# A two-layer linear-attention and SwiGLU kernel: the first row tile's keys by one fp32 product, four row tiles turned by TensorE, and new engine orders

## The chip, the cores and the metric

The kernel runs on one core of a Trainium2 chip. The metric is device time in microseconds for one execution, lower is better. The time before is 1136.47 us, the median of three runs (1135.8 to 1136.66).

## The reference

x has 2048 rows of 512. Two layers, each an attention block and a gated MLP, with the same weights in both layers:

```python
x = x + A(layernorm(x), wqkv, wo)     # linear attention, 32 heads of 16
x = x + B(layernorm(x), w1, w3, w2)   # silu(x@w1) * (x@w3) @ w2, 1792 hidden
# twice; in A:
pq, pk = phi(q), phi(k)               # phi(t) = (t+1 if t>0 else exp(t)) + 1e-6
kv  = einsum("bhsd,bhse->bhde", pk, v);  z = pk.sum over s
num = einsum("bhqd,bhde->bhqe", pq, kv); den = einsum("bhqd,bhd->bhq", pq, z) + 1e-6
out = (num / den) @ wo
```

All is fp32 in the reference.

## The kernel before

**Numbers as pairs.** A fp32 operand is held as two half-precision parts, high and low, after a scaling by a power of two. `mm` (L942) makes a product in three passes, `PASSES = ((0,0),(1,0),(0,1))`: high by high, low of the left by high, high of the left by low. Thus a 128 x 512 product over 512 inputs (four blocks k) is 12 matmuls of 512 columns. `split` (L835) makes the two parts of a weight: high on ScalarE, then low on VectorE.

**Scale of a weight.** `weight_scale` (L801): maxima of four pieces (`abs_max`, L788), a reduction (L805), a fp32 matmul against the identity into the bank `pm_k` (L808) to get the maximum over partitions, a reduction out of it (L810), a floor (L811), a scale (L813), and `flip_pow2` (L821), which turns it into the inverse power of two. Only then may `split` run.

**Row tiles.** The 2048 rows are 16 tiles of 128. Tile t needs its row statistics (`ln_stats`, VectorE L909 and L910, then four small GpSimd operations L917 to L921), `normalise` (ScalarE L924), a high part (ScalarE or GpSimd), a low part (a subtraction, GpSimd or VectorE), and it must be turned, so that its 512 inputs stand on the partitions. Tiles 0 and 1 are turned on TensorE (`first_tile`, L2342: four matmuls against the identity for each part into a bank `turn`, which ScalarE copies out, L2357); tile 2 by a transposing DMA (L939), all later ones by such a DMA in `keys_turn` (L1851, DMA L1858). All DMAs are issued on SP, whose order is fixed as well.

**Keys.** In `attention` (L1355), for each tile: the product of the turned tile with the keys' weights into a bank `pk` (12 matmuls), phi (`phi_act` L1333: Relu, Identity and Exp on ScalarE, where Identity writes back into the bank, so that the bank stays taken; `phi_sum` L1347: add and maximum on VectorE, L1350), the result's two parts (ScalarE L1396, VectorE L1405), and, a tile or two later, `gram`: 12 matmuls into the banks `gt`, which gather keys by rows over all tiles. Queries, the MLP, and a second layer that works on pairs of tiles follow.

**Banks.** PSUM's eight banks are two pools of four: `acc` (the `gt` and other sums) and `w` (tiles of ones, turns, `pm_k`, `pk`). A tile of the pool `w` can be written only when one of the four is free: when the last reader of what it held is done.

**Start.** Before the weights are there, `keep_busy` has TensorE multiply tiles of ones (L2369), 22 and later 3.

**Order.** The program is written in a plain order, and `arrange` then lays every engine's instructions out by a table `ORDER`: for each engine, the numbers of its instructions in program order, in the order in which they are to be issued. An engine issues strictly in that order, so an instruction that must wait holds all behind it. Nothing else sets the order.

Of the kernel before, what the change touches and what calls it, by code (L numbers as in the profile page):

```python
# [17 lines left out]
P = 128  # L18
# [477 lines left out]
def kernel(  # L496
# [833 lines left out]
    DEEP = 4  # L1330


    def phi_act(ps, u, eps, in_bank=False):  # L1333

# [1121 lines left out]
```

## Time and profile before

| | us |
|---|---|
| median of three runs | 1136.47 |
| span of the profiled execution | 1134.0 |
| outside the span, to the median | 2.5 |
| TensorE busy | 1123.7 (99%) |
| VectorE, ScalarE, GpSimd busy | 849.3, 663.2, 429.7 |
| TensorE's granted clock, mean | 0.999 |

A profile row gives start and length in us, the engine (PE is TensorE, DVE VectorE, ACT ScalarE, POOL GpSimd, SPq the queue of SP), the line of the kernel, the operation, out<-in by tile names, the shapes and a count; the bracket tells how long the engine was idle before it and what ended that. A row with a count is a run of equal instructions. A wait row reads: who waited, for whom, us in total, times, the longest. A row of a stretch gives its length and then, for TensorE, its weight loads, VectorE, ScalarE and GpSimd, the busy time with the count of instructions, the granted clock, the DMA engines' share and GB/s. A row of groups gives busy us and mean ns; a row of one tile gives shortest, median and longest duration in ns and the first and last start; a row of DMA issues gives KB and us from issue to landing.

### The profile page before, as it was taken

What the parts mean: (1) busy time and instruction counts of PE and PEld (TensorE: products, weight loads), DVE (VectorE), ACT (ScalarE), POOL (GpSimd) and SP (SyncE); (2) the same over time, 40 slices, a digit from 0 to 9 for tenths busy, and PEclk for the clock granted to TensorE, in tenths of its full rate; (3) what the DMA queues carried; (4) which work ended last, traced back from release to release, by engine and by line L of the source; (5) the groups of instructions that cost most, each with busy time, mean ns of one, the idle gap of its engine ahead of it and who ended that gap; (6) DMA issues with size and microseconds to landing.
All of it is one profiled execution on the core that took longest, in us unless ns stands there. A gap on an engine that the chain in (4) does not pass through costs nothing.

```text
span 1134.0 us, 22473 instructions
## 1 busy us (share of the span) xinstructions
PE 1123.7 (99%) x9117; PEld 888.3 (78%) x9117; DVE 849.3 (75%) x1468; ACT 663.2 (58%) x1104; POOL 429.7 (38%) x477
## 2 busy tenths in 40 slices
PE   8999999999999999999999999999999999999998
PEld 3445446888888888888886676578888888888887
DVE  7789878896978887889896488847855666465556
ACT  7668878775544445455578666686544434343442
POOL 6731796502001222335678416862152110302113
PEclk9999999999999999999999999999999999999999
DMA  8995665389673332331267946643482440220001
GB/s 258 304 292 181 174 136 121 75 220 272 204 279 122 117 149 103 112 155 66 48 179 177 276 165 153 114 89 105 120 240 102 177 178 1 85 84 29 11 20 57
DMA packets 171768, 162.94 MB, mean 144 GB/s; under 512 B 139536, under 2 KB 147984, under 8 KB 167056
## 3 DMA queue, kind: packets, MB, share of 16 engines
q1 hardware_dynamic: 171664, 161.51, 48.7%
q8 instruction: 71, 1.16, 0.4%
q14 instruction: 33, 0.27, 0.1%
HBM read 80.08 MB, written 47.32 MB: 112 GB/s over the span
## 4 chain that ended last, share of the span: by engine, by line
PE 91%; DVE 2%; POOL 2%; DMA 2%; issue 1%; ACT 1%; SPq 0%; DVEq 0%; POOLq 0%; ACTq 0%
PE bb L947 26%; PE po L2097 20%; PE bc L947 13%; PE ba L947 6%; PE gt L947 6%; PE po L947 5%; PE pq L947 4%; PE pk L947 3%; PE po L2117 3%; DMA arena<-arena 2%; PE kb L947 1%; PE qb L947 1%; PE kc L947 1%; PE kv L947 0%; PE qc L947 0%
## 5 line engine op out<-in xcount | busy, mean ns | idle before, releaser
L947 PEld LDWEIGHTS <-arena 128*128 128x128 f16 x6648 | 646.1, 98 | 204.5 <-DMA arena<-arena 4.4
L947 PE MATMUL bb<-arena 128*128 128x256 f16 x2688 | 349.2, 273 | 0.0
L2097 PE MATMUL po<-arena 128*128 128x256 f16 x2058 | 288.5, 273 | 0.0
L2052 ACT ACTIVATE arena<-bb 128x512 f32<-128x512 f32 x196 | 115.3, 594 | 195.5 <-PE bb L947 166.7
L2097 PEld LDWEIGHTS <-arena 128*128 128x128 f16 x2058 | 201.3, 98 | 23.4
L947 PE MATMUL bc<-arena 128*128 128x256 f16 x1344 | 179.6, 273 | 0.0
L2055 DVE TENSOR_TENSOR arena<-arena,bc 128x512 f32<-128x512 f32 x112 | 76.7, 685 | 87.5 <-PE bc L947 54.1
L2007 ACT ACTIVATE arena<-arena,scalars 128x512 f32<-128x512 f32 x112 | 74.6, 666 | 90.2 <-DVE arena L2055 70.2
L2146 DVE SCALAR_TENSOR_TENSOR arena<-po,scalars,arena 128x256 f32<-128x256 f32 (+1 forms) x180 | 101.5, 585 | 31.7 <-PE po L2097 21.7
L2013 DVE TENSOR_TENSOR arena<-arena 128x1280 f16<-128x1280 f32 (+1 forms) x90 | 105.4, 1174 | 21.2 <-ACT arena L2011 20.8
L2011 ACT ACTIVATE arena<-arena 128x512 f16<-128x512 f32 (+1 forms) x112 | 101.0, 904 | 32.2 <-DVE arena L2026 13.7
L2008 DVE SCALAR_TENSOR_TENSOR arena<-arena,scalars 128x512 f32<-128x512 f32 x112 | 78.6, 705 | 34.5 <-ACT arena L2007 34.4
L947 PE MATMUL ba<-arena 128*128 128x256 f16 x672 | 91.8, 273 | 0.0
L947 PE MATMUL gt<-arena 128*128 128x512 f16 x384 | 89.6, 379 | 0.0
L947 PE MATMUL po<-arena 128*128 128x512 f16 x384 | 86.8, 379 | 0.5 <-DMA arena<-arena 0.5
L2013 POOL TENSOR_TENSOR arena<-arena 128x512 f16<-128x512 f32 x22 | 27.0, 1228 | 115.0 <-ACT arena L2011 108.2
L2155 POOL TENSOR_TENSOR arena<-arena 128x512 f32<-128x512 f32 x27 | 38.0, 1406 | 81.7 <-DVE arena L2146 81.7
L2154 POOL TENSOR_TENSOR arena<-arena 128x512 f32<-128x512 f32 x27 | 37.1, 1375 | 71.4 <-DVE arena L2146 69.3
L871 DVE SCALAR_TENSOR_TENSOR arena<-arena,scalars 128x512 f16<-128x512 f32 (+2 forms) x74 | 59.1, 814 | 2.3 <-ACT arena L869 2.2
L924 ACT ACTIVATE arena<-arena,nb_all,rs_all 128x512 f32<-128x512 f32 x64 | 50.8, 806 | 13.2 <-POOL nb_all L921 7.6
L2023 POOL TENSOR_TENSOR arena<-arena 128x256 f32<-128x256 f32 x10 | 7.9, 786 | 131.3 <-DVE arena L2008 131.3
L869 ACT ACTIVATE arena<-arena,scalars 128x512 f16<-128x512 f32 (+2 forms) x74 | 52.2, 718 | 5.2 <-DVE arena L1003 2.3
(234 smaller groups left out, 1449.4 us busy)
## 6 DMA issues: line engine op xcount, KB each, us to landing
arena<-xb_d SPq DMA_DIRECT2D x12, 1792.0 KB, 8.0
xb_d<-arena SPq DMA_DIRECT2D x8, 1792.0 KB, 7.7
w_d<-arena SPq DMA_DIRECT2D x5, 1792.0 KB, 7.6
arena<-w_d SPq DMA_DIRECT2D x5, 1792.0 KB, 8.0
arena<-in_B_w_dram SPq DMA_DIRECT2D x8, 896.0 KB, 7.0
arena<-in_B_w_dram SPq DMA_DIRECT2D x28, 256.0 KB, 3.0
xt_d<-arena SPq DMA_DIRECT2D x8, 896.0 KB, 5.1
arena<-xt_d SPq DMA_DIRECT2D x8, 896.0 KB, 6.7
```

What stands on the lines that cost most here:

```text
L869: nc.scalar.activation(hi, src, AF.Copy, scale=scale)
L871: lambda: nc.vector.scalar_tensor_tensor(lo, src, scale, hi, OP.mult, OP.subtract)
L924: nc.scalar.activation(dst, x_sb[:, t, :], AF.Identity, scale=rs_all[:, t : t + 1], bias=nb_all[:, t : t + 1],)
L947: nc.tensor.matmul(dst, lhs(a, k), rhs(b, k), start=first and k == 0 and i == 0, stop=last and k == n - 1 and i == len(PASSES) - 1, skip_g ...
L2007: nc.scalar.activation(t, gate, AF.Silu, scale=info["u1"])
L2008: nc.vector.scalar_tensor_tensor(t, up, info["hid"], t, OP.mult, OP.mult)
L2011: nc.scalar.activation(hs[:, 0, lo:hi], t[:, lo:hi], AF.Copy)
L2013: engine.tensor_tensor(hs[:, 1, lo:hi], t[:, lo:hi], hs[:, 0, lo:hi], OP.subtract)
L2052: nc.scalar.activation(dst, bank_, AF.Copy)
L2055: nc.vector.tensor_tensor(dst, dst, bank_, OP.add)
L2097: nc.tensor.matmul(po[:, i * HALF : (i + 1) * HALF], hs[:, a, qx, cs], w2[:, b, qw, :], start=g == ends[0] and i + a + b == 0, stop=g == e ...
L2146: nc.vector.scalar_tensor_tensor(dst, src, cb, to, OP.mult, OP.add)
```

## The change

- **Loads.** The row tiles 0 to 3 are fetched ahead of the keys' weights (before: 0, 2, 1, the weights, 3), and then a block of w1 (896 KB).
- **Tile 0.** Its normalised fp32 rows are turned by four fp32 matmuls against the identity, ScalarE copies the result to `first["x"]`, and `first_product` multiplies it with the unscaled fp32 weights: four fp32 matmuls of 512 columns into the bank `pk`. Phi then uses the constant 1/SX as its scale. The pairs of tile 0, flat and turned, that later steps need are made by `first_parts`: two copies on ScalarE, two subtractions on GpSimd. The scale of the weights is still needed for all other tiles.
- **Tiles 1 to 3** are turned by TensorE (`TURNED = 4`); the banks are copied out by ScalarE for tile 1 and by VectorE for tiles 2 and 3.
- **Split of the keys' weights.** The high part of pieces 1 and 3 is made by VectorE instead of ScalarE.
- **Passes.** For tiles 1 to 3 `mm` puts the passes with the tile's low part last.
- **Scale.** Floor and scaling are one operation; the floor of the kept maximum comes after the flip.
- **Ones.** 20 and then 6 tiles of ones instead of 22 and 3.
- **ORDER** is new for all five queues, from the first instruction to the last.

The numbers in `ORDER` that matter at the start, after the change, by program order. TensorE: 0-19 and 24-29 ones, 20-23 tile 0's turn, 30-33 its fp32 product, 34 `pm_k`, 35-42, 43-50, 51-58 the turns of tiles 1, 2, 3 (four for the high part, then four for the low), 59-70, 83-94, 107-118, 131-142 the key products of tiles 1 to 4, 71-82 the first `gram`. VectorE: 13-16 maxima, 17, 18 reductions, 19 scale, 20 flip, 21 floor, 25-30 what it does of the split (26 and 29 high parts), 38 and 39 the copies of tile 2's turns, 42 tile 0's `phi_sum`, 43 and 44 tile 4's statistics, 46 and 48 the copies of tile 3's turns, 47 tile 3's low part. ScalarE: 2 the copy of tile 0's turn, 7 and 8 splits, 11 and 12 in `first_parts`, 13-15 phi of tile 0, 18-20 phi of tile 1, 22 and 23 tile 4's normalisation and high part. GpSimd: 15 and 20 the low parts of tiles 1 and 2, 21 and 22 the subtractions of `first_parts`, 31 tile 3's high part. SP: 0, 1, 6, 7 rows, 2-5 weights, 21 the block of w1, 18 and 8 rows 6 and 7, 16 the store of turned tile 0, 10 and 9 rows 5 and 4.

```diff
 ORDER = { "PE": (
-        "0-20 22-23 26-27 24 28 25 30 29 34 38-39 35-36 21 31-32 37 40-41 33 42-65 78-89 66-77 "
+        "0-17 20-23 18-19 24-28 30 34 29 35-39 43-46 40 31 41 47-50 42 32-33 51 55 52 59 "
+        "53-54 56 60 57-58 61-63 83-84 64 85-86 65 87-90 66 91-92 67-70 107-108 71 74 77 75 "
+        "109 80 78 76 93 110-111 81 94 112-115 72 79 116 101 98 73 95 82 102 117 104 96 103 "
+        "118 105 99 106 97 125 119 128-129 131-135 100 126-127 136-139 120 122-123 130 121 "
...
     "DVE": (
-        "1 7 9-10 16-17 23-24 11 14 13 12 15 36 18-21 37 39 25-28 40 31 22 29 4 32 46 33-34 2 5 "
+        "4 1 9-12 23-24 40 7 41 15 13-14 16-19 21 33 20 22 38 26 39 47 25 27-29 31 34 32 35 "
+        "30 36 5 42 46 43 52 44 53 45 54 48 55 49 61 51 66-67 50 62 56 60 73-74 70 59 63 65 "
...
     "Activation": (
-        "1-2 0 5-6 13-14 3-4 9-12 7-8 19 15-17 24 18 20 25 21 26 22 27 23 29 28 34 31 33 40 30 37 "
+        "0-1 3-4 2 11 9-10 5 17 7 6 8 13-15 12 16 18 20 19 22-23 21 24-28 32 29-31 38 33 35 "
...
     "Pool": (
-        "0-2 7 9 6 8 10 12-14 17 15 19 18 20 11 16 21-23 26 24-25 27-28 36 32 34 29-30 33 37 39 "
+        "1 0 2 6-9 11 10 13 12 18 14 16-17 23 19 24 15 21 25-26 20 31 37 22 32 27 29 28 30 49 "
...
     "SP": (
-        "0 6 5 3 1 4 2 7 19 9 28 8 10 15 24 16-17 20 18 21 23 22 25 34 53 26 40 29 52 30 32-33 27 "
+        "0-1 6-7 4 2-3 5 21 18 8 37 16 55 10 9 22 42 26 17 20 15 19 23-24 50 41 28 34 32 27 "
...
+        e, s = scalar(), scalar()
+        nc.vector.tensor_scalar(s, m, 2.0**-60, 2.0 / top, op0=OP.max, op1=OP.mult)
+        flip_pow2(s, s)
         nc.vector.tensor_scalar(m, m, 2.0**-60, None, op0=OP.max)
-        e, s = scalar(), scalar()
-        nc.vector.tensor_scalar(s, m, 2.0 / top, None, op0=OP.mult)
-        flip_pow2(s, s)
...
+        if low_last:
+            parts.sort(key=lambda part: part[1] == PASSES[1])
...
-            pp = bank("pk")
-            mm(pp, lambda a, k: xt[:, a * NK + k, :], lambda b, k: wk_s[:, b, k, :], NK)
+            pp = bank("pk") if t else first["pp"]
+            if t:
+                mm(
+                    pp,
+                    lambda a, k: xt[:, a * NK + k, :],
+                    lambda b, k: wk_s[:, b, k, :],
+                    NK,
+                    low_last=t < TURNED,
+                )
...
-            e, r = phi_act(pp, info["uk"], True)
+            if t == 0:
+                e, r = phi_act(pp, 1.0 / SX, True, neg=-1.0 / SX)
+            else:
+                e, r = phi_act(pp, info["uk"], True, neg=info["nuk"])
...
+    first = {}
+    TURNED = 4
+
+    def turned(t, nat, xt, a):
+        turn = bank(f"turn{a}")
+        for k in range(NK):
+            at = slice(k * P, (k + 1) * P)
+            nc.tensor.matmul(turn[:, at], nat[:, a, at], ident16, start=True, stop=True)
+        flat = xt[:, a * NK : (a + 1) * NK, :].rearrange("p k n -> p (k n)")
+        if t < 2:
+            nc.scalar.activation(flat, turn, AF.Copy)
+        else:
+            nc.vector.tensor_copy(flat, turn)
+
+    def first_product():
+        first["pp"] = pp = bank("pk")
+        for k in range(NK):
+            nc.tensor.matmul(
+                pp,
+                first["x"][:, k * P : (k + 1) * P],
+                st_att[1][:, k, :],
+                start=k == 0,
+                stop=k == NK - 1,
+            )
...
         high_part("key", t, nat[:, 0, :], xn)
+        if t < TURNED:
+            turned(t, nat, xts[t], 0)
         engine_of("keylow", t).tensor_tensor(nat[:, 1, :], xn, nat[:, 0, :], OP.subtract)
-        last["t"] = nc.sync.dma_start_transpose(xts[t], nat.rearrange("p a d -> p (a d)"))
+        if t < TURNED:
+            turned(t, nat, xts[t], 1)
+        else:
+            last["t"] = nc.sync.dma_start_transpose(xts[t], nat.rearrange("p a d -> p (a d)"))
...
-    x_piece(0, 1)
+    x_piece(0, 2)
     att_piece(1)
-    x_piece(1, 2)
     x_piece(2, 4)
...
+        if t == 0:
+            turn = bank("turn")
+            for k in range(NK):
+                at = slice(k * P, (k + 1) * P)
+                nc.tensor.matmul(turn[:, at], xn[:, at], ident, start=True, stop=True)
+            first["x"] = xf = f32()
+            nc.scalar.activation(xf, turn, AF.Copy)
+            first["later"] = (xn, nat, xt)
+            return
...
+    def first_parts():
+        xn, nat, xt = first["later"]
+        flat = xt.rearrange("p (a k) n -> p a (k n)", a=2)
+        for to, src in ((flat, first["x"]), (nat, xn)):
+            nc.scalar.activation(to[:, 0, :], src, AF.Copy)
+            nc.gpsimd.tensor_tensor(to[:, 1, :], src, to[:, 0, :], OP.subtract)
...
-        keep_busy(22)
+        keep_busy(20)
         ln_stats(0, 1)
+        first_tile(0)
+        keep_busy(6)
+        ln_stats(1, 1)
+        first_product()
...
         for k in range(NK):
-            split(wk_s[:, 0, k, :], wk_s[:, 1, k, :], st_att[1][:, k, :], scale)
+            hi, src = wk_s[:, 0, k, :], st_att[1][:, k, :]
+            if k % 2:
+                nc.vector.tensor_scalar(hi, src, scale, None, op0=OP.mult)
+            else:
+                nc.scalar.activation(hi, src, AF.Copy, scale=scale)
+            nc.vector.scalar_tensor_tensor(
+                wk_s[:, 1, k, :], src, scale, hi, OP.mult, OP.subtract
+            )
...
         first_tile(2)
+        first_parts()
```

More of the change, by code (lines that the diff above doesn't have):

```diff
@@ L940, in ln_tile, with mm @@
         return nat
-    def mm(dst, lhs, rhs, n, first=True, last=True, shared=False):
-        for k in range(n):
-            for i, (a, b) in enumerate(PASSES):
-                nc.tensor.matmul(
-                    dst,
-                    lhs(a, k),
-                    rhs(b, k),
-                    start=first and k == 0 and i == 0,
-                    stop=last and k == n - 1 and i == len(PASSES) - 1,
-                    skip_group_check=shared,
-                )
+    def mm(dst, lhs, rhs, n, first=True, last=True, shared=False, low_last=False):
+        parts = [(k, p) for k in range(n) for p in PASSES]
+        if low_last:
+            parts.sort(key=lambda part: part[1] == PASSES[1])
+        for i, (k, (a, b)) in enumerate(parts):
+            nc.tensor.matmul(
+                dst,
+                lhs(a, k),
+                rhs(b, k),
+                start=first and i == 0,
+                stop=last and i == len(parts) - 1,
+                skip_group_check=shared,
+            )
     w_rows = {n: w.rearrange("(c k p) n -> p c k n", p=P, k=2)
@@ L1330, with phi_act @@
     DEEP = 4
-    def phi_act(ps, u, eps, in_bank=False):
+    def phi_act(ps, u, eps, in_bank=False, neg=None):
         e, r = f32("kept"), ps if in_bank else f32()
         if eps:
-            nc.scalar.activation(e, ps, AF.Relu, scale=info["nuk"])
+            nc.scalar.activation(e, ps, AF.Relu, scale=neg)
             nc.scalar.activation(r, ps, AF.Identity, scale=u, bias=one_eps)
@@ L1849 @@
     xns = {}
+    first = {}
[13 more added lines that the diff above has]
+        for k in range(NK):
+            nc.tensor.matmul(
+                pp,
[4 more added lines that the diff above has]
+            )
     def keys_turn(t, xts, nats):
@@ L2343, in first_tile @@
         xt = ready[0][t] = xk_ring.next(F16, 2 * NK, P)
-        if t > 1:
+        if t >= TURNED:
             ready[1][t] = ln_tile(t, xt, engine)
@@ L2349, in first_tile @@
         nat = ready[1][t] = ring["nat"].next(F16, 2, D)
-        def turned(a):
-            turn = bank(f"turn{a}")
+        if t == 0:
+            turn = bank("turn")
             for k in range(NK):
                 at = slice(k * P, (k + 1) * P)
-                nc.tensor.matmul(turn[:, at], nat[:, a, at], ident16, start=True, stop=True)
-            flat = xt[:, a * NK : (a + 1) * NK, :].rearrange("p k n -> p (k n)")
-            nc.scalar.activation(flat, turn, AF.Copy)
+                nc.tensor.matmul(turn[:, at], xn[:, at], ident, start=True, stop=True)
[3 more added lines that the diff above has]
+            return
         nc.scalar.activation(nat[:, 0, :], xn, AF.Copy)
-        turned(0)
+        turned(t, nat, xt, 0)
         engine.tensor_tensor(nat[:, 1, :], xn, nat[:, 0, :], OP.subtract)
-        turned(1)
+        turned(t, nat, xt, 1)
+    def first_parts():
[4 more added lines that the diff above has]
+            nc.gpsimd.tensor_tensor(to[:, 1, :], src, to[:, 0, :], OP.subtract)
     warm = bank("warm")
@@ L2382 @@
             abs_max(parts[:, k : k + 1], st_att[1][:, k, :])
-        first_tile(0)
-        for i, _ in enumerate(weight_scale("k", parts, 2.0**14)):
-            if i == 0:
-                ln_stats(1, 1)
-            if i == 1:
-                keep_busy(3)
+        for _ in weight_scale("k", parts, 2.0**14):
+            pass
         first_tile(1)
@@ L2393 @@
         for k in range(NK):
-            split(wk_s[:, 0, k, :], wk_s[:, 1, k, :], st_att[1][:, k, :], scale)
+            hi, src = wk_s[:, 0, k, :], st_att[1][:, k, :]
[5 more added lines that the diff above has]
+                wk_s[:, 1, k, :], src, scale, hi, OP.mult, OP.subtract
+            )
         info["uk"] = scaled(e, 2.0**-23)
```

774 rows, old and new, of the table ORDER are left out of this document.

## The prediction

> **What bounds the kernel now.** I read the engine shares first, then stretches of the span, then TensorE's waits, then the head in order of time.
>
> ```profile
> PE 1123.7 (99%) x9117; PEld 888.3 (78%) x9117; DVE 849.3 (75%) x1468; ACT 663.2 (58%) x1104; POOL 429.7 (38%) x477
> ```
> ```profile
> 0.00:13.67 13.67, 9.83 (x45) 4.44 (x46) 8.15 (x22) 8.49 (x14) 8.31 (x24) 1.00 0.81 288
> 13.67:130.00 116.33, 116.03 (x580) 55.30 (x580) 100.77 (x208) 88.84 (x159) 51.26 (x99) 1.00 0.86 247
> 130.00:600.00 470.00, 470.00 (x4003) 391.59 (x4001) 398.07 (x697) 287.22 (x493) 188.68 (x189) 1.00 0.50 147
> 600.00:740.00 140.00, 137.70 (x945) 90.04 (x944) 101.87 (x167) 94.95 (x149) 78.81 (x72) 1.00 0.69 175
> 740.00:1130.00 390.00, 390.00 (x3550) 346.94 (x3547) 239.64 (x376) 183.68 (x291) 102.57 (x96) 1.00 0.29 92
> 1130.00:1134.00 4.00, 0.13 (x2) 0.00 (x0) 0.75 (x1) 0.00 (x0) 0.04 (x1) 0.77 0.43 162
> ```
> ```profile
> PE kb L947 <- DMA arena<-arena: 0.8, 1, 0.8
> PE kc L947 <- DMA arena<-arena: 0.6, 1, 0.6
> PE po L947 <- DMA arena<-arena: 0.5, 1, 0.5
> PE qc L947 <- ACT arena L1634: 0.3, 1, 0.3
> ```
>
> TensorE is the bound (second number of each stretch). From 13.67 to 1130 it idles 0.30 us before 130 and 2.3 us around the second layer's start, and nowhere else. So the end is: when the dense stream starts, plus its work, plus these few waits, plus a tail of 3.9. Only work taken out of the stream, or a stream that starts earlier or with holes, moves the time. The stream's start:
>
> ```profile
> 1.11 7.00 PE L2369 MATMUL warm<-ones 128*128 128x512 f16 x21 [1.11 <-DVE scalars L732]
> 7.95 0.28 PE L2355 MATMUL turn<-arena 128*128 128x128 f16 x2
> 10.46 0.45 PE L2355 MATMUL turn<-arena 128*128 128x128 f16 x5 [2.23 <-POOL arena L2361]
> 10.75 0.44 PE L808 MATMUL pm_k<-arena,scalars 128*128 128x128 f32 x2
> ...
> 13.67 7.54 PE L947 MATMUL pk<-arena 128*128 128x512 f16 x34 [0.18 <-DVE arena L837]
> 21.05 2.75 PE L947 MATMUL gt<-arena 128*128 128x512 f16 x12
> ...
> 26.23 2.75 PE L947 MATMUL gt<-arena 128*128 128x512 f16 x12
> 29.29 2.76 PE L947 MATMUL pk<-arena 128*128 128x512 f16 x12 [0.30 <-DMA arena<-arena]
> ```
> ```profile
> 7.51 2.49 DVE L789 TENSOR_REDUCE parts<-arena 128x1 f32<-128x512 f32 x4 [0.21 <-DMA arena<-in_A_wqkv_dram]
> ...
> 11.22 0.29 DVE L810 TENSOR_REDUCE scalars<-pm_k 128x1 f32<-128x128 f32 x1 [0.43 <-PE pm_k L808]
> ...
> 11.92 0.15 DVE L821 TENSOR_SCALAR scalars<-scalars 128x1 int32<-128x1 int32 x1
> ...
> 12.87 2.74 DVE L837 SCALAR_TENSOR_TENSOR arena<-arena,scalars 128x512 f16<-128x512 f32 x4
> ...
> 18.59 0.69 DVE L1857 TENSOR_TENSOR arena<-arena 128x512 f16<-128x512 f32 x1 [0.34 <-POOL arena L861]
> 19.20 0.68 DVE L1350 SCALAR_TENSOR_TENSOR arena<-arena 128x512 f32<-128x512 f32 x1
> ```
>
> The weights' absolute maxima (7.51 to 10.0) feed the scale (ready 12.07), the scale feeds the four splits (12.87 to 15.6), and the key products of tiles 0, 1, 2 (36 matmuls of 12 per tile) run behind them. A matmul of 512 columns starts every (7.54-0.38)/33 = 0.217 us, 0.38 being the overlap of one with the next. Tile 2's product thus starts at 21.05 - 12 x 0.216 = 18.46. The wait before tile 4's product costs 29.29 - 26.23 - 2.59 = 0.47 us.
>
> **The change, part by part.** (1) *Work.* Out go 12 half-precision key matmuls (2.59 us) and 8 turns of tile 0. In come four fp32 products, four fp32 turns, 16 turns for tiles 2 and 3. An fp32 matmul is two instructions:
>
> ```profile
> 96.45 1.02 PE L1434 MATMUL pz<-arena,scalars 128*128 128x512 f32 x2
> 97.31 1.03 PE L947 MATMUL gt<-arena 128*128 128x512 f16 x4
> ```
> ```profile
> L1457 PE MATMUL pz<-scalars,arena x8: 167/250/250, 106.4 to 107.7; 128*128 128x1 f32 x8
> ```
> 512 columns take 97.31 - 96.45 = 0.86 us, so the product takes 3.44, more than the 2.59 it replaces; but it needs no scale and no split, and so stands ahead of the stream. The fp32 turns are eight instructions at 0.13 (pm_k's pair: 11.02 - 10.75 = 0.27) to 0.19 (x8: 1.3/7): 1.0 to 1.5, I take 1.2. Sixteen turns at (0.45-0.22)/4 = 0.06: 0.9, also ahead of the stream.
>
> (2) *When the scale is ready.* The transfers now run x0 to x3, then the weights; the last weight piece takes the slot that a row tile had:
>
> ```profile
> 4.08 5.03 SPq L2319 DMA_DIRECT2D arena<-in_A_x_dram  x8
> ```
> ```profile
> arena<-in_A_x_dram SPq DMA_DIRECT2D x1, 256.0 KB, 5.4
> ```
> It lands at 4.08 + 5.4 = 9.5; its maximum and the reduction end at 10.35 (10.2 before). On TensorE 18 tiles of ones end at 7.95 - 3 x 0.216 = 7.3, the fp32 turns at 8.5, seven more tiles of ones at 10.0, the first quarter of the fp32 product at 10.9; only then pm_k, written behind it, may run (10.75 before). The scale follows 12.07 - 10.75 = 1.32 later, at 12.2: +0.15. That a maximum is moved behind the flip saves nothing, as two small operations stand in its place.
>
> (3) *What VectorE now does between the scale and the first phi sum.* This decides. In the new order it runs 22, 38 (copy of tile 2's high turn out of its bank), 26, 39 (copy of the low turn), 47 (tile 3's low part), 25, 27, 28, 29, four small ones, 30, two small ones, 42. By program order 25, 27, 28, 30 are the low parts of the split, 26 and 29 the two high parts moved here from ScalarE, and 42 is tile 0's phi sum. The phi of keys works in the bank (ScalarE's Identity writes back into it), so 42 is what frees tile 0's bank. TensorE has four banks for this: in its new order the product of tile 2 (83 on) comes after five matmuls of tile 1 (59 to 63), and then tile 0's product, tile 3's two turns (46 and 48, behind 42) and tile 1's product hold all four. So matmul 83, and the whole in-order stream behind it, waits for 42.
>
> ```profile
> L821 DVE TENSOR_SCALAR arena<-pz 128x512 int32<-128x512 int32 x2 | 1.4, 686 | 2.3 <-PE pz L1775 2.3
> ```
> ```profile
> 9.24 2.27 POOL L2361 TENSOR_TENSOR arena<-arena 128x512 f16<-128x512 f32 x2
> ```
> A copy out of a bank by VectorE isn't in the trace; its nearest row is this one-input 0.69, 0.60 from start to start as in the maxima (2.49 = 3 x 0.60 + 0.69). For 26 and 29 (one input, from memory) the bounds are the 0.15 of a one-column operation and 0.69; I take 0.60. The low copy 39 waits for tile 2's low part on GpSimd, now third in a row of 1.15 us subtractions (tile 1's, tile 0's new flat low part, tile 2's), which start at 8.5 and 9.7 to 10.3, and end with it at 12.5 to 13.0; TensorE's second quarter of the product (0.86) lies in front of the turn too, so 39 starts at about 13.5. From there: 0.60 (39) + 0.60 (47) + 3 x 0.665 (25, 27, 28; 2.74 = 3 x 0.665 + 0.74) + 0.60 (29) + 0.40 + 0.665 (30) + 0.20 + 0.69 (42) = 5.75, so 83 starts at **19.25**. TensorE's own way there ends earlier: the last half of the product (1.72) runs from 13.4 and is through at 15.4, 63 is issued at 16.4; ScalarE's relu, identity and exp of tile 0 end at 17.4. TensorE idles from 16.7 to 19.25. Bounds: with 39 not held (38 from 12.3) and 26, 29 at 0.15, 18.35; with the fp32 turns at their dear end, 19.6.
>
> [...]
>
> (4) *The account.* At 19.25 seven matmuls of tile 1 are still to do that before were done when tile 2 started, 1.51 us. Against 18.46: 19.25 - 18.46 + 1.51 = +2.30. Tile 4's wait (0.47) goes, since its product comes 58 matmuls after 83, at 31.8, instead of 28.8. Sum: **+1.83**. Without the replacement of tile 0's product, (3) would cost 2.59 more.
>
> (5) *What costs nothing, and why.* ScalarE loses two splits and gains copies; its cover is the wait in (3). SP loses two transposes, on which TensorE did not wait. A block of 896 KB now precedes x6, and x5, x4 stand behind the store of tile 0's turned rows (GpSimd, 11.5); they land near 16.5 (an estimate: four pieces of 256 KB at the 288 GB/s of the first stretch, 0.9 us each, and the landing), and VectorE first reads them after 42 and 46, at 19.9. Uncovered, a late x4 would cost its lateness. The orders behind the head are new for all engines; in TensorE's, the groups around the four waits quoted above stand as before (the kb group behind 21 gt matmuls, in other sequence), so I leave their 2.3 us.
>
> The sum is for the span, 1134.0; the runs' median 1136.47 lies 2.5 above it, and I add to the median: **1138.3**.
>
> **The rivals.** *A, no bank wait:* tile 2's product finds another bank, or 42 comes early. Then tile 1 starts at 15.4, with 8 turns (0.44) in it, level with the 21.05 - 24 x 0.216 = 15.87 of before, and only the 0.47 is won: 1136.0. For it: the new order puts 83, 84 ahead of 64, which needs only the third split; against it: the count of banks above.
>
> *B, the new orders take up the waits of the second layer:* all 2.2 us of them gives 1136.1; against it stands that three are on DMA landings, with the same TensorE groups ahead. *A and B together:* 1133.8, the only way I see to a faster kernel.
>
> *C, tile 4 comes late (slower):* its chain now starts behind tile 1's relu, as ScalarE's order puts relu, exp and identity of tile 1 ahead of tile 4's normalisation.
>
> ```profile
> 17.26 0.67 ACT L1339 ACTIVATE arena<-pk,scalars 128x512 f32<-128x512 f32 x1
> 17.83 0.77 ACT L1340 ACTIVATE arena<-pk,scalars 128x512 f32<-128x512 f32 x1
> 18.49 0.62 ACT L1341 ACTIVATE arena<-arena 128x512 f32<-128x512 f32 x1
> 19.01 0.81 ACT L924 ACTIVATE arena<-arena,nb_all,rs_all 128x512 f32<-128x512 f32 x1
> ```
> ```profile
> 22.75 1.26 SPq L1858 DMA_TRANSPOSE arena<-arena  x1
> ```
> ```profile
> arena<-arena SPq DMA_TRANSPOSE x1, 6.5
> ```
> Tile 1's product ends 17 matmuls after 83, at 23.1; five ScalarE steps (3.3) and the low part (0.7) later the transpose is issued, at 27.1. With the 6.5 us that tile 4's took before, it lands at 33.6, 1.8 after the 31.8 where TensorE wants it: 1140.1. It decides from 4.7 us of landing on. Against it: no 896 KB block is under way then, as one was before.
>
> *D, the clock falls (slower):* 21 tiles of ones take 6.62 us to their last start where 20 x 0.216 is 4.3, so a TensorE that comes from rest loses 2.3 us; after the 2.23 us idle at 8.2 it ran at full rate (0.06 a turn). If the longer idle of 2.55 before 83 is over the limit, 2.3 are lost: 1140.6. [...]
>
> **How the numbers follow.** Forecast 0.50 (its own range 1137.4 to 1138.7, from the bounds of (3)); A 0.14; B 0.12; A with B 0.07; C 0.11; D 0.06. The range 1135.0 to 1140.5 leaves out A with B and most of D. A measurement of this kernel tells 0.2%, 2.3 us, from no change: faster is below 1134.2, slower above 1138.7. Faster: A with B and an edge of A and B, 0.11. Slower: C, D and the upper part of the forecast, 0.27. The rest, 0.62, is no change.
>
> **What would show it.** Right: an idle of 2 to 3 us on TensorE between some five key matmuls of the second tile and the next, ended by VectorE's phi sum (add and max, L1350 before); the reduction out of pm_k at 11.3; dense TensorE from about 19.2; no wait at tile 4. The forecast is wrong if TensorE is dense from 15.5 on (A), if a key product waits for a transpose near 32 (C), if matmuls of 512 columns start 0.43 apart after the wait (D), or if the waits of the second layer differ by over 1 us (B).

## The result and the profile after

The changed kernel takes **1143.66 us** (median of six runs, 1140.64 to 1146.86) against 1136.78 for the kernel before beside it (six runs, 1135.8 to 1138.1): ratio 1.0060, 95% interval 1.0047 to 1.0074. It is 0.6% slower, and lies above the predicted range. The profiled execution, on which the rows below rest, took 1146.86 us, span 1145.1; it is the slowest of the six. The profile of the kernel before has a span of 1134.0, as its fastest runs do (a run takes 1.7 us more than its span). So the two profiles differ by 11.1 us where the medians differ by 6.9: the rows tell where time goes, the medians how much it is. Of all runs below one, of the kernel m2, took 1469.83 us at a granted clock of 0.751 and is left out; all others had 0.996 or more.

The first line of the page, and TensorE's longest waits in the view of waits (us in total, times, longest):

```profile
PE 1130.4 (99%) x9130; PEld 889.8 (78%) x9130; DVE 859.6 (75%) x1474; ACT 661.1 (58%) x1102; POOL 438.8 (38%) x478
```
```profile
PE po L950 <- DMA arena<-arena: 2.7, 2, 2.3
PE pk L950 <- DMA arena<-arena: 2.2, 1, 2.2
PE po L2140 <- DVE arena L2189: 1.4, 1, 1.4
```

Before, the longest of these was 0.8 us; now there are two of over 2 us on turned tiles, one of 1.4, and many small ones. The head, the work up to row tile 4, is not where the loss comes from. TensorE there, in order of time (start, length, what, how many, the idle time before it):

```profile
13.47 1.94 PE L1881 MATMUL pk<-arena 128*128 128x512 f32 x4
...
15.41 0.38 PE L950 MATMUL pk<-arena 128*128 128x512 f16 x1
...
16.12 4.91 PE L950 MATMUL pk<-arena 128*128 128x512 f16 x22
20.87 1.03 PE L950 MATMUL gt<-arena 128*128 128x512 f16 x4
...
29.29 1.24 PE L950 MATMUL pk<-arena 128*128 128x512 f16 x5
```

From 15.4 on it is dense: no wait ahead of tile 2's product, the first gt product at 20.87 (21.05 before), and no wait ahead of tile 4's at 29.29 (0.46 before).

**A sum that carries the rest.** Take TensorE's matmuls in order of start. Where one starts later behind the one before it than its shape's spacing (216 ns for 512 columns, 109 for 256, 56 for 128), the excess is lost; I add the excesses over 0.12 us from 14 us on. The span less this sum is nearly one number for every kernel of this study (1129.2 to 1131.2), so the time is this sum. The three highest, e2, m3 and m4, lost some 1 us more just ahead of where the sum begins, m3 by a wait, e2 and m4 by a lower granted clock (last section). (Us, of the profiled executions; the last four columns say where it is lost. The labels are explained with the experiments.)

| kernel | span | lost | span less lost | 14 to 120 | 120 to 215 | 215 to 600 | from 600 |
|---|---|---|---|---|---|---|---|
| before | 1134.0 | 4.3 | 1129.7 | 0.5 | 0.0 | 0.2 | 3.7 |
| after | 1145.1 | 15.6 | 1129.6 | 3.7 | 4.6 | 3.3 | 4.1 |
| e1 | 1147.6 | 18.0 | 1129.6 | 14.2 | 0.0 | 0.0 | 3.8 |
| e2 | 1147.2 | 16.4 | 1130.8 | 5.9 | 3.1 | 3.0 | 4.5 |
| e3 | 1148.5 | 18.9 | 1129.6 | 2.4 | 12.6 | 0.9 | 3.0 |
| e4 | 1141.3 | 11.7 | 1129.6 | 2.4 | 2.9 | 3.7 | 2.7 |
| e5 | 1143.6 | 13.8 | 1129.8 | 2.4 | 3.3 | 4.1 | 4.0 |
| p1 | 1141.6 | 12.2 | 1129.4 | 2.9 | 2.5 | 4.5 | 2.3 |
| m1 | 1138.5 | 9.1 | 1129.4 | 0.7 | 1.3 | 4.7 | 2.4 |
| m2 | 1133.9 | 4.7 | 1129.2 | 0.5 | 0.0 | 0.2 | 4.0 |
| m3 | 1150.1 | 18.8 | 1131.2 | 4.2 | 4.8 | 4.4 | 5.4 |
| m4 | 1137.9 | 7.3 | 1130.6 | 0.0 | 0.0 | 0.2 | 7.2 |
| x1 | 1141.5 | 11.8 | 1129.7 | 1.8 | 6.8 | 0.0 | 3.2 |
| x2 | 1136.0 | 6.5 | 1129.4 | 2.5 | 0.6 | 0.2 | 3.2 |

The new program has no more to do on its critical path than the old one (1129.6 against 1129.7). The 11.2 us by which its sum is larger are late starts, nearly all in the first 600 us, but none before 38 us, and so none in the head; 1.7 us of them are slow matmuls, of which more below.

How one of the large ones comes about shows in SyncE's issues of the changed kernel:

```profile
74.88 0.56 SPq L964 DMA_DIRECT2D arena<-in_B_w_dram  x1
75.48 0.91 SPq L1918 DMA_DIRECT2D xt_d<-arena  x2
76.43 1.70 SPq L2369 DMA_DIRECT2D arena<-in_A_wqkv_dram  x2
83.51 1.24 SPq L1901 DMA_TRANSPOSE arena<-arena  x1
```

The transpose at 83.51 waits for the first store of 75.48, as the view of SyncE's waits says:

```profile
SPq L1901 <- DMA xt_d<-arena: 5.3, 1, 5.3
```

That store was issued just behind 896 KB of weights and landed at 83.45. TensorE wanted the turned tile at 84.3 and got it at 86.6:

```profile
83.65 0.81 PE L950 MATMUL gt<-arena 128*128 128x512 f16 x3
86.64 1.68 PE L950 MATMUL pk<-arena 128*128 128x512 f16 x7 [2.18 <-DMA arena<-arena]
```

The other one, at 138.95, cost more than itself. TensorE, then the stretch behind it (the figure ahead of the last two is the granted clock):

```profile
135.16 1.46 PE L950 MATMUL po<-arena 128*128 128x512 f16 x6
138.95 4.45 PE L950 MATMUL po<-arena 128*128 128x512 f16 x12 [2.34 <-DMA arena<-arena]
```
```profile
140.00:144.00 4.00, 4.00 (x13) 1.46 (x11) 0.56 (x1) 3.94 (x14) 3.19 (x3) 0.60 0.44 120
```

Twelve matmuls take 4.45 us there, where e4 below has 2.76 for the same twelve: 1 us after the wait eight follow at 427 ns instead of 216, 1.69 us more.

### The profile page after: what moved, and what is told of

The parts are those of the page before. It is cut to its first block, busy times and chain, and to the rows that moved or that the text cites. A ratio compares the mean times of both kernels' runs of the same rounds, so it can differ in the third digit from the quotient of the medians.

```text
span 1145.1 us, 22484 instructions
## 1 busy us (share of the span) xinstructions
PE 1130.4 (99%) x9130; PEld 889.8 (78%) x9130; DVE 859.6 (75%) x1474; ACT 661.1 (58%) x1102; POOL 438.8 (38%) x478
## 4 chain that ended last, share of the span: by engine, by line
PE 74%; DVE 6%; POOL 3%; ACT 3%; issue 2%; DMA 2%; SPq 0%; DVEq 0%; POOLq 0%; ACTq 0%
PE bb L950 23%; PE po L2140 18%; PE bc L950 11%; PE ba L950 5%; PE po L950 5%; PE gt L950 3%; PE po L2160 2%; PE pq L950 2%; PE kb L950 2%; DMA arena<-arena 1%; PE qb L950 1%; DMA arena<-in_B_w_dram 1%; PE kc L950 1%; POOL arena L1772 1%; DVE arena L2098 1%
## 5 line engine op out<-in xcount | busy, mean ns | idle before, releaser
L950 PEld LDWEIGHTS <-arena 128*128 128x128 f16 x6636 | 644.4, 98 | 211.0 <-DMA arena<-arena 10.6
L2050 ACT ACTIVATE arena<-arena,scalars 128x512 f32<-128x512 f32 (+1 forms) x112 | 74.5, 665 | 95.3 <-DVE arena L2098 86.2
L2051 DVE SCALAR_TENSOR_TENSOR arena<-arena,scalars 128x512 f32<-128x512 f32 (+1 forms) x112 | 85.0, 761 | 49.6 <-ACT arena L2050 49.3
L2189 DVE SCALAR_TENSOR_TENSOR arena<-po,scalars,arena 128x256 f32<-128x256 f32 (+1 forms) x180 | 100.3, 584 | 23.4 <-PE po L2140 13.2
L926 ACT ACTIVATE arena<-arena,nb_all,rs_all 128x512 f32<-128x512 f32 x64 | 50.9, 806 | 12.4 <-POOL nb_all L923 6.7
```

What stands on the lines that cost most here:

```text
L926: nc.scalar.activation(dst, x_sb[:, t, :], AF.Identity, scale=rs_all[:, t : t + 1], bias=nb_all[:, t : t + 1],)
L950: nc.tensor.matmul(dst, lhs(a, k), rhs(b, k), start=first and i == 0, stop=last and i == len(parts) - 1, skip_group_check=shared,)
L2050: nc.scalar.activation(t, gate, AF.Silu, scale=info["u1"])
L2051: nc.vector.scalar_tensor_tensor(t, up, info["hid"], t, OP.mult, OP.mult)
L2189: nc.vector.scalar_tensor_tensor(dst, src, cb, to, OP.mult, OP.add)
```

## The experiments

My theory after the result: the head is what rival A said, and the loss is the new written order behind it. The rival: the changed head (other transfers, more work on VectorE) delays what follows, whatever the order.

### The order cut at row tile 4 (e1, e2)

```diff
 # e1, the changed program, each engine's list
-  tiles 0 to 3: changed order   from tile 4: changed order
+  tiles 0 to 3: changed order   from tile 4: order before (PE +5, DVE +6, ACT -2, POOL +1, SP -2)
 # e2, the program before
-  tiles 0 to 3: order before    from tile 4: order before
+  tiles 0 to 3: order before    from tile 4: changed order
```

> The changed program with the written order cut in two: up to row tile 4 each engine's list is the changed one, from there on the work stands in the order of the kernel before (the numbers shifted by what the head adds or drops; TensorE's, ScalarE's and SyncE's rests are in the old order exactly, some 14 neighbours differ on VectorE and 2 on GpSimd). Theory (the loss sits in the new order behind the head, the head itself wins what the lost wait of tile 4 was): the head of the changed kernel runs 0.2 us ahead at the first gt product and has no 0.46 us wait at tile 4, so this runs 0.6 us under the kernel before, about 1136.2 us by 1136.8. Rival (the new head itself, its loads in another order and its 6 more VectorE operations, delays what follows): it stays near the changed kernel, 1141 to 1144, with waits at 86 and 139 us again. My prediction's own third step (the phi sum holds the bank) would give +1.8, 1138.6.

> The mirror image: the program of the kernel before, its own order up to row tile 4, and behind that the order of the changed kernel. Theory: it has the loss without the change of the head, 0.6 us over the changed kernel, about 1144.3, with the waits near 86 and 139 us and the halved matmuls behind the second. Rival (the head causes it): within 1 us of the kernel before, 1136 to 1138.

e1: 1149.64 us, ratio 1.0105 (1.0092 to 1.0119). e2: 1148.98, ratio 1.0101 (1.0085 to 1.0116). Both far over either parent: neither theory had that. The table shows where: behind 120 us e1 loses 3.8 us, as the kernel before does, but 14.2 ahead of it. e2 is the mirror of that: behind 120 us the new order loses 10.6 us in the old program, nearly as much as in the changed one (11.9). So it brings most of its late starts there without the changed head. The largest piece of e1's loss, in e1's VectorE in order of time and in TensorE's waits:

```profile
62.02 0.68 DVE L791 TENSOR_REDUCE parts<-arena 128x1 f32<-128x512 f32 x1
69.97 1.09 DVE L791 TENSOR_REDUCE pt_w<-arena 128x1 f32<-128x896 f32 x1 [7.27 <-DMA arena<-in_B_w_dram]
```
```profile
PE gt L950 <- DVE arena L1417: 6.1, 3, 5.4
PE pk L950 <- DMA arena<-arena: 3.2, 2, 1.7
```

An early maximum of a later weight stands in VectorE's list where its transfer used to have landed; here the transfer is issued at 62.97 and lands at 69.95, and the whole queue of VectorE stands 7.3 us behind it. Ahead of that, VectorE has less room. The stretch from 16 to 38 us in the kernel before and in the changed kernel (the third busy time is VectorE's):

```profile
16.00:38.00 22.00, 21.70 (x102) 9.68 (x100) 16.47 (x39) 17.51 (x28) 15.66 (x45) 1.00 1.02 278
```
```profile
16.00:38.00 22.00, 22.00 (x105) 10.04 (x104) 19.75 (x44) 16.18 (x26) 16.20 (x39) 1.00 0.84 250
```

Of 22 us it is busy 19.75 instead of 16.47. So the rival may have a part in it: with the new head, the early part of the old order does not fit any more; which of the two makes the transfer late was not tried apart. A cut at tile 4 can't tell the two apart, because what it measures is mostly the seam, the place where the two orders were joined.

### The order cut behind the first attention (e3)

> The changed kernel with its own order as far as the first layer's attention goes (190 us on TensorE), and the order of the kernel before from the first product of the feed-forward part on. It splits the loss. Theory: the starts of TensorE's matmuls of the changed kernel lose about 7.7 us between 38 and 144 us and 7.3 us behind that, where the kernel before loses 3.7 us; so about 3.5 us of 7 come back, 1140 us, and the waits of 2.3 and 2.5 us at 86 and 139 us are still there. Rival (a late part shifts everything behind it, the second half of the loss follows from the first): no change, 1143 to 1144.

1149.48 us, ratio 1.0106 (1.0092 to 1.0119). Far slower again, with 12.6 us lost between 120 and 215: 8.1 of them from 183 us on, at the seam, and 4.5 around a wait at 137.8 that the changed kernel has too (2.89 us here, 2.50 there, both with slow matmuls behind).

```profile
PE po L951 <- DMA arena<-arena: 5.7, 3, 2.7
PE bc L951 <- DVE arena L2099: 1.9, 1, 1.9
```

But from 215 us on, where the old order runs undisturbed, the changed program loses 3.9 us with it, as the kernel before does (3.9), against 7.3 with its own. For that part the order alone is at fault, and not the head. The run shows one thing more. Up to 110 us all its lists are those of the changed kernel, and still TensorE waits 0.80 us at 84.96 where the changed kernel's profile has 2.35 at 86.64. So one order has waits of other sizes in other executions.

### Two entries of SyncE's list (e4, e5)

```diff
 # e4: SyncE's list (60 the weight load, 62 and 67 the stores)
-   64 77 61 60 62 67 14 12 66 13
+   64 77 61 62 67 60 14 12 66 13
 # e5: that, and the transpose 92 ahead of four loads
-   91 82 71 94 99 93 97 92 100 98 96 101
+   91 82 71 92 94 99 93 97 100 98 96 101
```

> The changed kernel with one entry of SyncE's list moved: the weight load issued at 74.88 us (917 KB, landed at 82.80) goes behind the two stores of turned tiles that were issued at 75.48 and 76.02 and landed at 83.45 and 84.09. The transpose issued at 83.51 had waited 6.9 us for the first of these stores. Theory (SyncE's order makes the wait): the store lands near 78, the transpose is issued by 79 and lands by 82, the wait of 2.35 us at 86.6 us is gone, and the time falls by about 2.3 us against the changed kernel, to 1141.3. Rival (the transfers of that stretch are the limit, and something else is late next): another wait of 1 to 2 us stands in its place and the time stays within 1 us of 1143.7.

> The kernel of the run before with the load behind the two stores, and on SyncE a second entry moved: the transpose issued at 132.98 us (landed 138.91, on which TensorE's first po matmul of that row tile waited 2.50 us) goes ahead of the weight pieces issued at 129.57, 131.61 and 131.99 and a load of stored tiles at 132.51; its source on GpSimd was ready at 129.75. Theory: it lands 3 us earlier, the wait of 2.5 us goes or falls under 0.5, and the 8 matmuls of 427 ns instead of 216 that followed it in one of the two profiles are not there; 2.0 to 2.5 us less than the run before, 1140.8 to 1141.3. Rival (the next transposes of the same group, landing at 140.4 and 141.3, are late next): about 1 us comes back, 1142.3.

e4: 1143.26 us, ratio 1.0052 (1.0039 to 1.0064), where the changed kernel has 1.0060: at most a little. SyncE in e4, and TensorE at the second wait:

```profile
75.19 1.05 SPq L1911 DMA_DIRECT2D xt_d<-arena  x2
76.28 0.45 SPq L957 DMA_DIRECT2D arena<-in_B_w_dram  x1
...
80.34 1.24 SPq L1894 DMA_TRANSPOSE arena<-arena  x1
```
```profile
137.81 2.76 PE L943 MATMUL po<-arena 128*128 128x512 f16 x12 [2.32 <-DMA arena<-arena]
```

The mechanism was as told: the first store lands at 78.3, the transpose is issued 3.2 us earlier, and the wait at 86.6 is gone. A wait of 0.2 us stands in its place at 88 (1.0 in e5), and the medians show no gain of 2.3. A second one, 0.8 us at 62, lies ahead of the moved entry and can't come from it. The wait at 138 is still 2.48 us (2.32 of them idle), and this time no slow matmuls follow.

e5: 1144.2 us, ratio 1.0068 (1.0056 to 1.0080): nothing won. The wait at 138 is gone, and TensorE, that much earlier, now waits for a load of stored tiles that SyncE issues at 153.04, behind a transpose it was held at from 150.23 to 152.99:

```profile
145.73 7.93 PE L943 MATMUL po<-arena 128*128 128x512 f16 x36
155.94 4.28 PE L943 MATMUL pq<-arena 128*128 128x512 f16 x19 [2.28 <-DMA arena<-xt_d]
```

The rivals of these two runs were right in kind, in e5 with a load in place of the next transposes: a single wait of this order isn't worth its length. In e5 the next one was due behind it. In e4 it may also be that the wait of 2.35 us, seen in the slowest execution, is shorter in most, as it is in e3; no run settles that.

### The order mended (m1, m2) and the bank really held (p1)

```diff
 # m1: TensorE's list as it is; 64 moves of single entries in the others, for example
-  SP   ... 233 stands at place 233      DVE ... 184 at place 172
+  SP   ... 233 at place 231             DVE ... 184 at place 171
 # m2: the same for the kernel before, 16 moves
 # p1: m1, and tile 0's phi in its bank
         e, r = f32("kept"), ps if in_bank else f32()
+        if in_bank == "first":
+            f32()
-                e, r = phi_act(pp, 1.0 / SX, True, neg=-1.0 / SX)
+                e, r = phi_act(pp, 1.0 / SX, True, in_bank="first", neg=-1.0 / SX)
```

In p1 the added `f32()` takes the buffer that is now not written, so that all later buffers stay the ones of m1.

> The program of the changed kernel, every operation as it was; in its written order 64 single entries stand one to a few places earlier or later (38 on VectorE, 9 on SyncE, 9 on GpSimd, 8 on ScalarE, none on TensorE), chosen with a replay of the trace's durations and dependencies so that operands come before TensorE asks for them. In the five profiles so far the span less what TensorE's matmuls start late after 14 us is 1129.6, 1129.6, 1129.6, 1129.6 (all four orders of the changed program) and 1130.8, and 1129.8 for the kernel before: the time is that sum. Theory (the loss is the new order's waits, the change of the program itself costs nothing): the waits fall from 15.5 us to 3 to 6, span 1132.6 to 1135.6, time 1134.4 to 1137.4, no slower than the kernel before. Rival (the changed head delays the work behind it, whatever the order): the waits return elsewhere and it stays above 1140.

> The kernel before, with 16 single entries of its order moved by the same means (5 on VectorE, 4 on SyncE, 4 on GpSimd, 3 on ScalarE). It shows what mending alone is worth where the program is not changed. Its waits are 4.2 us; theory: they fall by 1 to 2 us, time 1134.8 to 1135.8. If the mended order of the changed program comes out under this one, the change of the head is worth the difference, by the sums above 0.2 us and the wait of 0.46 us at tile 4; if it comes out over it, the change costs that much beside its order.

> The mended order of the changed program, with one thing changed: ScalarE writes the second half of tile 0's phi into tile 0's PSUM bank, not into SBUF, so that VectorE's sum reads it there and the bank stays held until that sum ends (18.94 us in the changed kernel's profile). It is the wait that my prediction put into the change and that the change does not have: matmul 83 was to start at 19.25 there, and started near 16.8. Theory: with the bank really held the wait is there, TensorE idles from 16.8 to about 19.0, the first gt product comes 2.2 us later, and the time is 1.8 to 2.3 us over the mended kernel. Rival (other tiles' matmuls or slack behind take it up): under 0.5 us.

m1: 1142.08 us, ratio 1.0044 (1.0032 to 1.0056). m2: 1136.24, ratio 0.9995 (0.9986 to 1.0004). Mending brings the changed program some 1.6 us, less than hoped, and the old one nothing that can be told from noise. In m1 the first 215 us lose 2.0 us instead of 8.2, so the head does not forbid a good order right behind it; but the stretch from 215 to 600 us, the first layer's MLP, loses 4.7.

p1: 1144.03 us, 1.95 over m1; ratio 1.0065 (1.0053 to 1.0077). TensorE in m1, then ScalarE's Identity and TensorE in p1:

```profile
15.99 4.93 PE L943 MATMUL pk<-arena 128*128 128x512 f16 x22
20.75 1.03 PE L943 MATMUL gt<-arena 128*128 128x512 f16 x4
```
```profile
15.79 0.66 ACT L1337 ACTIVATE pk<-pk,scalars 128x512 f32<-128x512 f32 x1
```
```profile
15.97 0.81 PE L943 MATMUL pk<-arena 128*128 128x512 f16 x3
18.91 4.26 PE L943 MATMUL pk<-arena 128*128 128x512 f16 x19 [2.12 <-DVE arena L1347]
23.00 1.03 PE L943 MATMUL gt<-arena 128*128 128x512 f16 x4
```

Identity now writes pk, and there is the wait of my prediction, at its place, with its releaser (L1347 is the phi sum there) and at 18.91 where I had 19.25: the start is 2.29 us late, and the time 2.0 us longer. So the mechanism and its price were sound; the changed kernel just doesn't hold the bank.

### Orders from a better replay (m3, m4)

The lists were searched with a replay of measured durations and dependencies; no short diff shows them.

> Again the changed program with TensorE's list as it is and the other four engines' lists mended, now with the replay fed from five profiles of this program (it gives 4.4 us of waits for the kernel before, 4.35 measured; 13.2 on the mean for the changed order, 13.9 measured without the 1.7 us of slow matmuls; 6.7 for the first mended order, 9.1 measured). The list it found has 4.6 us of waits in the replay, mended over the whole span: places in VectorE's list break at 275 points, ScalarE's 112, SyncE's 55, GpSimd's 54. Theory (the loss is the order's waits wherever they are): measured waits of 5 to 7 us, span 1134.6 to 1136.6, time 1136.4 to 1138.4, level with the kernel before within 0.2%. Rival (the changed head costs something that no order of the others mends): it stays at the 1142 us of the first mended order.

> The kernel before mended in the same way from its own two profiles (places break at 20, 28, 21 and 14 points): 2.6 us of waits in the replay against 4.4. Theory: 1 to 2 us less than the kernel before, 1135.0 to 1136.0. It is the counterpart of the run above: what mending the order gives without the change. Rival (the replay is not good enough at this size, as with the first mended order of this program, 0.9995): no change.

m3: 1151.6 us, ratio 1.0130 (1.0116 to 1.0144). m4: 1141.21, ratio 1.0038 (1.0025 to 1.0052). Both are worse than what they started from. m3's longest waits:

```profile
PE po L943 <- DMA arena<-arena: 2.1, 2, 1.8
PE pq L943 <- DMA arena<-xt_d: 2.1, 1, 2.1
```

The replay promised 4.6 us of waits and the chip gave 18.8; for the old program it promised 2.6 and the chip gave 7.3. For orders that had been measured the replay was nearer (4.4 for 4.3, 13.2 for 13.9, 6.7 for 9.1). That fits a search that picks just those orders of which the replay thinks too well; it was not tested. m4 matters for the question, because it is the program before with nothing changed but an order, and it loses 4.5 us. Its profile, 3.9 us longer than that of the kernel before, has 3.5 us more of late starts from 600 us on (7.2 against 3.7) and some 1 us from a lower clock in the head. A new order alone can cost several microseconds; this change cost 6.9.

### Two orders joined where it holds (x1, x2)

```diff
 # x1, the changed program: m1's order up to the query tiles 12 and 13, the order before behind
 # x2, the changed program: m1's order up to the first query tile, the order before behind
-  PE   561.. : changed order
+  PE   561.. : order before, each number + 5     (and so on the other four engines)
```

> The changed program, joined from two lists that each ran on the chip with few waits: up to the second-last query tiles of the first layer's attention the first mended order (waits of 1.3 us by its profile there), from row tile 12 of that part on the order of the kernel before, on all five engines (behind 215 us it had 3.0 us of waits in the changed program, 4.0 in its own), joined where the two orders' times differ by 3 us. It replaces the joint at 190 us, which alone cost 9 us of waits between 183 and 216. Theory (the program of the change costs nothing, the order of it does): 5 to 7 us of waits, span 1134.6 to 1136.6, time 1136.4 to 1138.4, level with the kernel before within 0.2%. Rival (the changed head costs more than its waits, or its earlier order leaves the old one late): over 1140.

> As the run before, with the joint placed at 120 us, ahead of the first query tile of the attention: first mended order up to there, order of the kernel before behind it, joined with 8 us. The part taken from the first mended order has 0.7 us of waits in its profile, the replay puts 1.8 us at the joint. Theory: 5 to 7 us of waits again, time 1136.4 to 1138.4; the less of the new order is left, the fewer waits. Rival: the attention of the changed program needs the new order (waits at 125 to 190 us), over 1140.

x1: 1141.06 us, ratio 1.0036 (1.0022 to 1.0049), with 6.8 us lost around its seam, between 120 and 215. x2: **1137.67 us, ratio 1.0005 (0.9996 to 1.0014)**, level with the kernel before. Its longest waits, and the stretch from 215 to 600 in the kernel before, in the changed kernel and in x2 (the first busy time is TensorE's):

```profile
PE pk L949 <- DMA arena<-arena: 1.4, 2, 0.7
...
PE po L949 <- DMA arena<-arena: 0.6, 2, 0.5
```
```profile
215.00:600.00 385.00, 385.00 (x3485) 340.82 (x3484) 329.26 (x558) 216.09 (x342) 123.61 (x124) 1.00 0.48 152
215.00:600.00 385.00, 383.02 (x3488) 340.89 (x3487) 330.85 (x559) 214.25 (x343) 126.21 (x118) 1.00 0.46 149
215.00:600.00 385.00, 385.00 (x3497) 341.95 (x3495) 329.37 (x559) 215.95 (x344) 123.56 (x123) 1.00 0.48 152
```

The same operations as the changed kernel, and 6.0 us less by the medians. Behind 120 us it loses 4.0 us, as the kernel before does (3.9), where the changed kernel loses 11.9. That settles the larger part: **with another order the changed program costs nothing that can be measured, so it is the new order that costs the 0.6%.** What x2 has over the kernel before is 2.1 us of waits ahead of 120 us, above all at 39.6 and 63.3. They can't come from the joint: up to 105 us all its lists are those of m1, and m1 lost 0.7 us in the same stretch, with no wait at these two places. So what the changed head itself costs is not settled; it was 0.3 us over the kernel before in m1 and 2.1 in x2, by one profile each.

No run beat the kernel before by more than its interval. Which engine's list does the most harm was not tried apart.

## Why the prediction was wrong

It gave 1138.3 with a range to 1140.5, for a reason that the chip does not have, and left out the one that it has.

**Steps 1 and 2 hold.** A quarter of the fp32 product takes 0.89 (two from 13.47 to 15.25), I had 0.86. The eight instructions of the fp32 turn take 0.90 (7.76 to 8.66), less than my 1.0 to 1.5. The flip that ends the scale is through at 12.4, I had 12.2.

**Step 3 failed at one sentence**, that the phi of keys works in the bank; my description of the kernel before says so too, and it is wrong for keys in both kernels. VectorE's own course was right to 0.3 us (start, length, operation):

```profile
12.34 0.68 DVE L1875 CAST arena<-turn 128x512 f16<-128x512 f32 x1
12.94 0.48 DVE L2446 TENSOR_SCALAR arena<-arena,scalars 128x512 f16<-128x512 f32 x1
13.62 0.69 DVE L1875 CAST arena<-turn 128x512 f16<-128x512 f32 x1 [0.20 <-PE turn L1870]
...
18.25 0.68 DVE L1352 SCALAR_TENSOR_TENSOR arena<-arena 128x512 f32<-128x512 f32 x1
```
```profile
15.94 0.68 ACT L1342 ACTIVATE arena<-pk,scalars 128x512 f32<-128x512 f32 x1
```

The first copy out of a bank takes 0.60 from start to start, the held low copy starts at 13.62 (I had 13.5), the phi sum ends at 18.9 (I had 19.25). But ScalarE's Identity reads pk and writes arena, so the bank is free at 16.6, and matmul 83 follows without a stop. The same row of before, L1340 `arena<-pk,scalars`, stands in my own prediction under rival C; it says in its output that Identity's result isn't in the bank. In the code only a call that asks for it writes into the bank, and this call does not. By p1 the step would have been worth 2.3 us of wait, had it been so.

**Step 4** put +1.83 where the head does what rival A said: 0.18 us are won at the first gt product and 0.46 at tile 4, some 0.6 us by 38 us.

**Step 5 is the one that decided.** "So I leave their 2.3 us" gave the new orders of five engines no cost, where they cost nearly all of the 6.9 us that the medians show, because TensorE's groups around four old waits stood as before. But whether an operand is there when TensorE asks for it is set by the other lists as well: with TensorE's list the same to the last entry, the late starts are 9.1 us in m1, 15.6 in the changed kernel and 18.8 in m3. Measured, they go from 4.3 to 15.6 us with the change; e3 behind 215 us and x2 behind 120 us show that they go away with the old order, and m4 that a new order alone brings some. That the time moved up, as my sum had it, is luck: the wait behind that sum did not occur.

**The rivals.** A was right on the head and wrong on the sum, since it too left the orders. B's waits of the second layer hardly moved in total (3.7 to 4.1 from 600 us on). C did not come: tile 4 is there in time. D's falling clock came, though at 139 us and not at matmul 83, and cost 1.7 us (granted clock 0.60 from 140 to 144 us); the wait of 2.29 us in p1, at the place that I had in mind, did not bring it. That an idle of 2.55 us is safe, on which D's small chance rested, was not shown: the trace of before has 2.23 us without a fall, and in the changed kernel a fall followed 2.50. For each of the two scalings on VectorE (26 and 29) I took 0.60 us; measured, one takes 0.48, 0.40 from start to start (16.81 to 17.21), against 0.68 and 0.60 for the copy out of a bank.

## What to carry to other kernels

When a change rewrites the order of every engine, price the order as a part of its own: sum TensorE's late starts before, ask for each large operand in the new lists what its queue does ahead of it, and give the case "the orders fit worse" a size of several such waits, not the size of the ones seen before. Don't tell the gain of one mended wait from one profile, since the same lists gave 0.80 us in one execution and 2.35 in another. Look at the output of the row that you say holds a bank. And an order found on a model has to be chosen by runs: one that promised 4.6 us of waits had 18.8.

## What the runs showed of the hardware

**The clock after a short idle.** TensorE's starts after waits of 2.2 to 2.9 us were followed by one stretch of seven or eight matmuls at 427 ns in some places and not in others: yes after 2.50 (after), 2.89 (e3), 2.24 (m3), 2.45 (x1); no after 2.35 (after), 2.48 (e4), 2.65 (e3, a second place), 2.44 (e5), 2.39 (m4) and 2.29 (p1). In e3 one also followed two shorter waits in a row, 2.11 at 198.2 and 1.22 at 200.1 us, and the 5.52 us of e1 were followed by ten slow matmuls. In the head of the kernel before, 2.23 us of idle ahead of the turns had no slow matmuls behind; in e2 and m4, at the same place, 2.64 and 2.80 us had (granted clock 0.53 from 13 to 16 us and 0.55 from 10.5 to 14.3). The clock of x1 and e5, the idle stretch first:

```profile
179.00:181.40 2.40, 0.11 (x2) 0.09 (x2) 2.33 (x5) 0.57 (x3) 2.40 (x4) 1.00 1.01 209
181.40:186.00 4.60, 4.60 (x14) 1.69 (x15) 4.57 (x12) 3.57 (x8) 2.13 (x2) 0.63 1.13 166
```
```profile
153.00:156.00 3.00, 0.72 (x5) 0.16 (x3) 2.96 (x6) 3.00 (x7) 2.92 (x5) 1.00 0.53 134
156.00:160.00 4.00, 4.00 (x19) 1.82 (x20) 3.83 (x8) 1.37 (x4) 3.86 (x5) 1.00 0.33 63
```

So the length of the idle alone does not decide between 2.2 and 2.7 us; what does was not tested. In these runs such a wait cost its length, or, with seven or eight matmuls at 427 ns instead of 216 behind it, 1.5 to 1.7 us more.

**The spread.** The changed kernel's runs spread over 6.2 us, those of the kernel before over 2.3 beside it. That fits the many waits, of other sizes in other executions, and the clock above, but it was not tested.
